# A two-bank PSUM tile split into two tiles, and 4500 added to the planned landing of a narrow job's x and sums

## The chip, the cores and the metric

The kernel runs on one core of one Trainium2 chip. The metric is device time in microseconds (us) of one execution, as the median of a few runs. Engine names are those of the profile: PE is TensorE's matmul row, PEld its weight loads, DVE VectorE, ACT ScalarE, POOL GpSimd, and SP the queue that issues every DMA of this kernel.

## The reference

Attention of 4 batches of 8 heads (576 positions, head size 64) with a decay and a causal mask feeds a block with a squared ReLU, and that feeds a block with a normalised softmax-linear unit.

```python
scores = scale * np.matmul(q, k.transpose(0, 1, 3, 2))
decay = cum[:, :, :, None] - cum[:, :, None, :]          # cum: running sum of log f
attn = softmax(where(causal, -1e9, scores + decay))
x = matmul(attn, v)                                      # to 2304 tokens x 512
h = x @ w_in                                             # 2304 x 2048
x = (s * relu(h) ** 2 + b) @ w_out                       # 2304 x 512
h = x @ w2_in                                            # 2304 x 1024
sm = softmax(h); solu = h * sm
out = (layernorm(solu) * g_ln) @ w2_out
```

## The kernel before, in words

All matrix products take float32 operands split in a high and a low part, so one product is three matmuls. The work has three stages. In the first, 16 pairs of heads go through attention: scores into PSUM (L663), minimum and exponent on DVE and ACT (L704, L750), transposes (L765), the product with v (L834). The results are stored as `xs_d`, not yet divided by the softmax sums; the inverse sums go to `rs_d`. In the second stage, the block with the squared ReLU runs in jobs. Five narrow jobs (`job`, L1076) take 256 tokens each and three of the eight slices of the hidden width; they lie between the attention's matmuls, since their matmuls have a later priority (1000 + 100 n, against the attention's running number). Wide jobs (`job_wide`, L1122) of up to 512 tokens do the rest after the attention. In the third stage pairs of tiles go through the last block (`pair2`, L1269, and `tile2_out`).

**A narrow job's input.** `x_load` (L946) issues for job n one DMA of x (512 KB, L963, into `xraw`) and two of the inverse sums, each broadcast over 64 partitions (256 KB each, L968, into `xo`, here called `rb`). A multiplication of 128x1024 elements (L971, issued by the helper at L428 or L429) joins them; it may go to DVE or POOL. Then come a store of the product (L972), the high part (L976) and the low part (L977), both written to `xhl`. `xraw`, `xo` and `xhl` each exist once, so the next job's transfers wait for this job's reads, and the next `xhl` waits for this job's first-layer matmuls (L1112, output `h`). The first narrow job (n = 0) loads in two halves.

**What sets the order.** The program records operations with `add` and then runs a planner (`Plan.run`). It plays the operations through in a modelled time, engine by engine, and writes each engine's instructions in the order in which the model starts them. On the chip each engine then works through its own list in that order and waits with semaphores. The model has a cost per operation and a lag per engine; for a transfer (L233 to L235) one modelled ring is busy for bytes over a rate, and the transfer counts as landed 900 after the ring is through, or 900 + `SLD` for those of later priority. The x and sums of a narrow job have the priority `min(b, BS)`, so they count as landed after 900. When a transfer counts as landed, its readers become ready, and an engine takes the ready operation with the least ready time plus priority. The model's times decide nothing else: no instruction waits for a clock.

**The PSUM tiles.** `hps` is one bank, `x2ps` (L364) a tile of two banks, [128, 4, 256] floats. Its halves have keys of their own in the planner, ("x2", 0, 0) and ("x2", 0, 1), so the planner treats them as independent. They serve as score banks and as targets of filler matmuls early in the attention, as the accumulator of the narrow jobs' second layer (copied out by ACT at L1101), as two of the four banks through which the wide jobs' first layer rotates (h, h1 and the two halves, L1128 to L1130; read by ACT's ReLU at L1046), and as two banks of the first `pair2`. The profile shortens both the names `x2` and, after the change, `x2h` by their numbers: the tile is `x` in the rows below. The semaphore waits themselves are set by the framework from the order of the recorded instructions and the tiles that they touch.

Of the kernel before, what the change touches and what calls it, by code (L numbers as in the profile page):

```python
# [8 lines left out]
F32 = mybir.dt.float32  # L9
# [9 lines left out]
CH = 256  # L19
# [5 lines left out]
BX = -3000  # L25
# [30 lines left out]
URGENT = -50000  # L56
SLD = 1500
SLP = 500
SLT = 100000
# [7 lines left out]
class Plan:  # L67
# [15 lines left out]

    def add(self, eng, dur, fn, r=(), w=(), pri=0, bytes=None, after=(), lk=False, rate=340, act=1.0, open=False, tiled=None, hold=0):


        ways = eng if isinstance(eng, dict) else {eng: (dur, fn)}
        ways = {e: (d[0], d[1], e == "POOL" or e == "DVE" and (lk or len(d) > 2 and d[2])) for e, d in ways.items()}
        op = dict(ways=ways, pri=pri, bytes=bytes, n=len(self.ops), succ=[], t=0.0, by=None, rate=rate, act=act, open=open, tiled=tiled, hold=hold, r=tuple(r), w=tuple(w))
        deps = set(after)  # L90
        for x in r:
            if x in self.writer:
                deps.add(self.writer[x])
        for x in w:
            if x in self.writer:
                deps.add(self.writer[x])
            deps.update(self.readers.pop(x, ()))
        for x in r:
            self.readers.setdefault(x, []).append(op["n"])
        for x in w:  # L100
            self.writer[x] = op["n"]
            self.readers.pop(x, None)
        deps.discard(op["n"])
        op["wait"] = len(deps)
        for d in deps:
            self.ops[d]["succ"].append(op["n"])
        self.ops.append(op)
        return op["n"]

    def run(self):  # L110
# [71 lines left out]
        while left:  # L182
# [4 lines left out]
            for eng in sorted(ready):  # L187
# [45 lines left out]
                if best["bytes"]:  # L233
                    ring = max(ring, t + 1300) + best["bytes"] / best["rate"]
                    end = ring + (900 if best["pri"] < BX or t < SLT else 900 + SLD)  # L235
                best["end"] = end
# [22 lines left out]
def act_p(n):  # L259
    return 51 + 0.833 * n  # L260
# [22 lines left out]
def kernel(  # L283
# [44 lines left out]
    w2_d = dram.tile([NB2, 2, 128, 1024], F32, name="w2_d")  # L328

    const = ctx.enter_context(tc.tile_pool(name="const", bufs=1))  # L330
    moe = ctx.enter_context(tc.tile_pool(name="moe", bufs=1))
# [4 lines left out]
    psa = att_st.enter_context(tc.tile_pool(name="psa", bufs=1, space=PSUM))  # L336

    def tiles(pool, shape, dt, name, n):
        return [pool.tile(shape, dt, name=f"{name}{i}") for i in range(n)]

# [22 lines left out]
    hps = [psm.tile([128, 2, CH], F32, name="h")]  # L363
    x2ps = [psm.tile([128, KD, CH], F32, name="x2")]  # L364

# [30 lines left out]
    spare = [(hps[0].rearrange("p u n -> p (u n)"), ("h", 0))]  # L396
    spare += [(x2ps[0][:, 2 * g:2 * g + 2].rearrange("p k n -> p (k n)"), ("x2", 0, g)) for g in range(2)]
    for x in ({"S": "S", "P": "PT", "O": "O"}[x] for x in SPARE):
# [14 lines left out]

    def dma(out, in_, r, w, size, pri=0, rate=340, after=()):
        add("SP", 600, lambda: nc.sync.dma_start(out=out, in_=in_), r, w, pri, bytes=size, rate=rate, after=after)

# [106 lines left out]

    P.fill = (WT, {("x2", 0, 1): zeros(x2ps[0][:, 2].rearrange("p (k n) -> p k n", k=2)), ("x2", 0, 0): zeros(x2ps[0][:, 0].rearrange("p (k n) -> p k n", k=2)), ("h", 0): zeros(hps[0][:, 0].rearrange("p (k n) -> p k n", k=2))})

# [420 lines left out]
    def x_load(n, c, src, hi, lo, khi, klo, b=BX):  # L946
# [6 lines left out]
        for g in range(2 if first else 1):  # L953
            ks = slice(2 * g, 2 * g + 2) if first else slice(0, KD)
            sz = (ks.stop - ks.start) * CH
            of = (lambda key: [key + (g,)]) if first else H
            kx, kh, kl = of(("xx", 0)), of(khi), of(klo)
            raw_, hi_, lo_ = xraw[:, ks], (lambda ks=ks: hi()[:, ks]), (lambda ks=ks: lo()[:, ks])
            if src is xs_d:
                view = xs_d[ks, :, cs].rearrange("k p t -> p k t")  # L960
                rk = [("xs", p, half) for p in range(NPAIR) for half, o, w in ((0, 0, 256), (1, 256, 320))
                      if p // PPB * S + o < t1 and p // PPB * S + o + w > t0 and ks.start <= p % PPB < ks.stop]
                dma(raw_, view, rk, kx, 512 * sz, min(b, BS))  # L963
                P.first = P.first or len(P.ops) - 1
                krb = [("xo", a, u) for a in range(2) for u in ((g,) if first else range(2))]
                rk = [x for k_ in rk for x in rs_keys(*k_[1:])]
                for a in range(2):
                    dma(rb[64 * a:64 * a + 64, ks], rs_d[ks, a, cs][None].broadcast_to((64, ks.stop - ks.start, CH)), rk,  # L968
                        [k_ for k_ in krb if k_[1] == a],
                        256 * sz, min(b, BS), rate=290)  # L970
                tt(lambda raw_=raw_: raw_, lambda raw_=raw_: raw_, lambda ks=ks: rb[:, ks], sz, ALU.mult, krb, kx, b)  # L971
                dma(xc_d[ks, :, cs].rearrange("k p t -> p k t"), raw_, kx, [("xc", c, k) for k in range(ks.start, ks.stop)],  # L972
                    512 * sz)
            else:
                dma(raw_, src[ks, :, cs].rearrange("k p t -> p k t"), [("x2d", c, k) for k in range(KD)], kx, 512 * sz, b)
            copy(hi_, lambda raw_=raw_: raw_, sz, kx, kh, b)  # L976
            tt(lo_, lambda raw_=raw_: raw_, lambda hi_=hi_: f32(hi_()), sz, ALU.subtract, kx + kh, kl, b)  # L977
# [98 lines left out]
    def job(n, c, fps, b=BMOE):  # L1076

        hi, lo, khi, klo = (lambda: xhis[0]), (lambda: xlos[0]), ("xx", 2), ("xx", 3)
        x_load(n, c, xs_d, hi, lo, khi, klo)
        kx2, x2, h, kh = ("x2", 0), (lambda: x2ps[0]), (lambda: hps[0]), ("h", 0)  # L1080
        for m, fp in enumerate(fps):
# [7 lines left out]
            for u in range(2):  # L1089
                for g in range(2):  # L1090
                    def x_mm(u=u, g=g, tb=tb, gh=gh, gl=gl, st=st, fin=fin):
                        for d in (2 * g, 2 * g + 1):
                            x_mms(x2()[:, d, :], tb, gh[:, u, :], gl[:, u, :], u, d, st and u == 0 and d % 2 == 0, fin and u == 1)

# [4 lines left out]
        for g in range(2):  # L1099
            a = slice(2 * g, 2 * g + 2)  # L1100
            add("ACT", act_p(512), lambda a=a: nc.scalar.copy(out=xo_[:, a], in_=x2()[:, a]), [kx2 + (g,)],  # L1101
                kxo[g], b)
# [19 lines left out]
    def job_wide(n, t0, width, fps, last, b=BMOE):  # L1122
# [6 lines left out]
        if x:  # L1129
            hbanks += [(lambda g=g: flat(x2ps[0][:, 2 * g:2 * g + 2]), ("x2", 0, g)) for g in range(2)]  # L1130
        work = [(m, fp, us) for m, fp in enumerate(fps) for us in ([(0,), (1,)] if x else [(0, 1)])]
# [137 lines left out]
    def pair2(g):  # L1269
# [3 lines left out]
        if g == 0:  # L1273
            banks = [(lambda i=i: late["x2w"][2 + i], ("x2w", 2 + i)) for i in range(2)]
            banks += [(lambda i=i: x2ps[0][:, 2 * i:2 * i + 2].rearrange("p k n -> p (k n)"), ("x2", 0, i)) for i in range(2)]
        else:
# [291 lines left out]
```

## Time and profile before

| | |
|---|---|
| Median of 3 runs | 793.2 us (791.77 to 794.97) |
| Profiled execution, own time | 794.93 us |
| Its span, first to last instruction | 792.9 us |
| Instructions | 12751 |
| PE busy | 773.7 us, 98% of the span |
| DVE, ACT, POOL busy | 476.5, 492.8, 132.7 us |
| Mean granted TensorE clock | 0.994 of full speed |

The span is cut in stages: attention with the narrow jobs from the start to about 272 us, wide jobs to about 589 us, the last block to the end. PE counts as busy in nearly all of it, so time is found by looking for the places where PE waits or where the granted clock is below 1.

### The profile page before, as it was taken

Reading aid. Unit: us, or ns where it says so; the run is one execution under the profiler, and the core shown is the slowest. Engines: PE = TensorE matmul, PEld = TensorE weight load, DVE = VectorE, ACT = ScalarE, POOL = GpSimd, SP = SyncE. Lnnn points to the kernel's source line nnn. Section 1 sums busy time; section 2 is a strip of 40 time slices with the busy share of each in tenths; the row PEclk is TensorE's granted clock in tenths of the full one; section 3 lists DMA queues with packets and bytes.
Section 4 is the critical chain, followed back from the end, with each engine's and each line's share of the span. In section 5 each row is a group of like instructions: output and inputs, shape, how many; then the busy total and the mean of one; then the engine's idle time right before and its main releaser. Section 6 shows DMA issues by size and latency. Waiting matters only on the chain.

```text
span 792.9 us, 12751 instructions
## 1 busy us (share of the span) xinstructions
PE 773.7 (98%) x4520; PEld 640.2 (81%) x4520; DVE 476.5 (60%) x1026; ACT 492.8 (62%) x1008; POOL 132.7 (17%) x180
## 2 busy tenths in 40 slices
PE   8998999899999999999999999999999999999998
PEld 6677788788788987888788888788997788888886
DVE  9999888688674573221378666512239966655530
ACT  7998888588777686555387676554516654443441
POOL 3332412123110020100111201100002730100000
PEclk9999999899999999999999999999999999999999
DMA  8886888886953873130467865842325121000011
GB/s 301 281 291 202 289 280 268 271 278 197 330 180 102 271 258 118 54 106 1 120 211 256 300 207 180 306 197 81 107 82 211 54 66 41 27 14 27 27 41 53
DMA packets 73015, 132.59 MB, mean 167 GB/s; under 512 B 7704, under 2 KB 29848, under 8 KB 72952
## 3 DMA queue, kind: packets, MB, share of 16 engines
q1 hardware_dynamic: 72952, 131.78, 49.6%
q8 instruction: 35, 0.57, 0.3%
q14 instruction: 28, 0.23, 0.1%
HBM read 91.17 MB, written 40.58 MB: 166 GB/s over the span
## 4 chain that ended last, share of the span: by engine, by line
PE 79%; DVE 9%; DMA 6%; issue 2%; ACT 2%; SPq 1%; POOL 0%; DVEq 0%; ACTq 0%; POOLq 0%
PE h L1112 14%; PE x L1112 9%; PE ph L1321 7%; PE x2w L1119 7%; PE x2w L1118 7%; PE x2w L1120 7%; PE po L1377 4%; PE po L1379 4%; PE po L1378 4%; PE S L663 4%; PE PT L765 3%; DMA xo<-rs_d 2%; PE O L834 2%; DVE e L704 2%; PE pt L1365 2%
## 5 line engine op out<-in xcount | busy, mean ns | idle before, releaser
L1060 DVE SCALAR_TENSOR_TENSOR gl<-r,b_sb,gh 128x512 fp32r<-128x512 f32 x71 | 54.4, 767 | 128.5 <-ACT gh L1069 114.6
L750 ACT ACTIVATE e<-e,m 128x256 f32<-128x256 f32 (+4 forms) x144 | 83.4, 582 | 10.2 <-DVE m L704 9.7
L1119 PE MATMUL x2w<-gl,u 128*128 128x512 f32 (+1 forms) x200 | 73.6, 368 | 0.0
L1120 PE MATMUL x2w<-gh,u 128*128 128x512 f32 (+1 forms) x200 | 73.6, 368 | 0.0
L1118 PE MATMUL x2w<-gh,u 128*128 128x512 f32 (+1 forms) x200 | 73.6, 368 | 0.0
L765 PE MATMUL PT<-ident,e 128*128 128x128 f32 x384 | 60.2, 284 | 3.7 <-ACT wr L869 1.3
L1046 ACT ACTIVATE r<-h 128x512 f32<-128x512 f32 x46 | 27.3, 593 | 53.7 <-PE h L1112 53.4
L1112 PE MATMUL h<-xhl,w 128*128 128x256 f32 (+1 forms) x384 | 60.0, 295 | 0.0
L1377 PE MATMUL po<-v,dh 128*128 128x512 f32 x144 | 58.2, 404 | 0.0
L1379 PE MATMUL po<-v,dl 128*128 128x512 f32 x144 | 56.3, 391 | 0.0
L765 PEld LDWEIGHTS PT<-ident,e 128*128 128x128 f32 x384 | 43.6, 143 | 15.6 <-issue 3.5
L1378 PE MATMUL po<-v,dh 128*128 128x512 f32 x144 | 56.1, 390 | 0.0
L1369 DVE TENSOR_TENSOR dl<-pt,dh 128x512 fp32r<-128x512 f32 x36 | 24.6, 689 | 49.5 <-ACT dh L1368 49.5
L1053 ACT ACTIVATE r<-r,s_sb 128x512 f32<-128x512 f32 x68 | 49.3, 725 | 2.2
L1112 PEld LDWEIGHTS h<-xhl,w 128*128 128x128 f32 x384 | 49.6, 190 | 1.2
L1112 PE MATMUL h<-xh,u 128*128 128x256 f32 (+1 forms) x216 | 46.0, 330 | 0.0
L1069 ACT ACTIVATE gh<-r,b_sb 128x512 fp32r<-128x512 f32 x62 | 44.7, 721 | 1.5 <-DVE r L1050 0.2
L1052 ACT ACTIVATE r<-r 128x512 f32<-128x512 f32 x68 | 43.0, 632 | 1.8
L1046 ACT ACTIVATE r<-x 128x512 f32<-128x512 f32 x26 | 15.5, 596 | 44.8 <-PE x L1112 44.8
L1118 PEld LDWEIGHTS x2w<-gh,u 128*128 128x128 f32 x200 | 37.7, 188 | 6.3
L1119 PEld LDWEIGHTS x2w<-gl,u 128*128 128x128 f32 x200 | 37.7, 189 | 6.2
L1120 PEld LDWEIGHTS x2w<-gh,u 128*128 128x128 f32 x200 | 37.7, 188 | 6.2
(280 smaller groups left out, 1972.4 us busy)
## 6 DMA issues: line engine op xcount, KB each, us to landing
wraw<-in_moe_w_in_dram SPq DMA_DIRECT2D x24, 512.0 KB
wraw<-in_moe_w_out_dram SPq DMA_DIRECT2D x24, 512.0 KB
w_d<-w SPq DMA_DIRECT2D x44, 256.0 KB
raw<-in_qk_dram SPq DMA_DIRECT2D x12, 608.0 KB
dec<-dec_d SPq DMA_DIRECT2D x12, 512.0 KB
v<-w_d SPq DMA_DIRECT2D x12, 512.0 KB
vs<-in_v_dram SPq DMA_DIRECT2D x16, 320.0 KB
u_d<-wr SPq DMA_DIRECT2D x20, 256.0 KB
```

Of the source, the lines that this page charges most:

```text
L750: nc.scalar.activation(out=e[:, c], in_=e[:, c], func=AF.Exp, scale=-1.0, bias=m[:, j:j + 1], accum_out=rt[:, cols[j]:cols[j] + 1])
L765: nc.tensor.transpose(pt[:, kb, :], e[:, 128 * kb:128 * kb + 128], ident)
L1053: nc.scalar.activation(out=r, in_=r, func=AF.Copy, scale=s_sb)
L1060: nc.vector.scalar_tensor_tensor(out=gl, in0=r, scalar=b_sb, in1=f32(gh), op0=ALU.add, op1=ALU.subtract)
L1112: nc.tensor.matmul(t, w_, v_[:, kc, :], start=kc == 0 and first and x == 0, stop=kc == KD - 1 and x == 2, skip_group_check=True)
L1118: nc.tensor.matmul(t, a_, gh, start=start, stop=False, skip_group_check=True)
L1119: nc.tensor.matmul(t, a_, gl, start=False, stop=False, skip_group_check=True)
L1120: nc.tensor.matmul(t, b_, gh, start=False, stop=stop, skip_group_check=True)
L1321: nc.tensor.matmul(o, s_[:, kc, :], mv[:, c], start=x < 5 and kc == 0 and z == 0, stop=kc == 1 and z == 2, skip_group_check=True)
L1377: nc.tensor.matmul(ot, dh[:, j, :], wh[:, c], start=j == 0, stop=False)
L1378: nc.tensor.matmul(ot, dh[:, j, :], wl[:, c], start=False, stop=False)
L1379: nc.tensor.matmul(ot, dl[:, j, :], wh[:, c], start=False, stop=j == 7)
```

## The change

It does two things. The two-bank tile `x2ps` becomes two tiles of one bank, `x2h0` and `x2h1`, with every use rewritten to the tile of its half. And `add` gets an argument `slack`, which the planner adds to the modelled landing of a transfer; for narrow jobs other than the first it is `SLX` = 4500 for the x and for both transfers of the sums. The instructions themselves, their sizes and their number of operands stay; the order in which the planner writes them may differ from the first of these transfers on.

```diff
+SLX = 4500
...
-    def add(self, eng, dur, fn, r=(), w=(), pri=0, bytes=None, after=(), lk=False, rate=340, act=1.0, open=False, tiled=None, hold=0):
+    def add(self, eng, dur, fn, r=(), w=(), pri=0, bytes=None, after=(), lk=False, rate=340, act=1.0, open=False, tiled=None, hold=0, slack=0):
...
                     ring = max(ring, t + 1300) + best["bytes"] / best["rate"]
-                    end = ring + (900 if best["pri"] < BX or t < SLT else 900 + SLD)
+                    end = ring + (900 if best["pri"] < BX or t < SLT else 900 + SLD) + best["slack"]
...
-    x2ps = [psm.tile([128, KD, CH], F32, name="x2")]
+    x2ps = tiles(psm, [128, 2, CH], F32, "x2h", 2)
...
-    spare += [(x2ps[0][:, 2 * g:2 * g + 2].rearrange("p k n -> p (k n)"), ("x2", 0, g)) for g in range(2)]
+    spare += [(x2ps[g].rearrange("p k n -> p (k n)"), ("x2", 0, g)) for g in range(2)]
...
-                dma(raw_, view, rk, kx, 512 * sz, min(b, BS))
+                late_ = 0 if first else SLX
+                dma(raw_, view, rk, kx, 512 * sz, min(b, BS), slack=late_)
...
-                        256 * sz, min(b, BS), rate=290)
+                        256 * sz, min(b, BS), rate=290, slack=late_)
...
-        kx2, x2, h, kh = ("x2", 0), (lambda: x2ps[0]), (lambda: hps[0]), ("h", 0)
+        kx2, x2, h, kh = ("x2", 0), (lambda d: x2ps[d // 2][:, d % 2]), (lambda: hps[0]), ("h", 0)
...
-            add("ACT", act_p(512), lambda a=a: nc.scalar.copy(out=xo_[:, a], in_=x2()[:, a]), [kx2 + (g,)],
+            add("ACT", act_p(512), lambda a=a, g=g: nc.scalar.copy(out=xo_[:, a], in_=x2ps[g]), [kx2 + (g,)],
...
-            hbanks += [(lambda g=g: flat(x2ps[0][:, 2 * g:2 * g + 2]), ("x2", 0, g)) for g in range(2)]
+            hbanks += [(lambda g=g: flat(x2ps[g]), ("x2", 0, g)) for g in range(2)]
...
-            banks += [(lambda i=i: x2ps[0][:, 2 * i:2 * i + 2].rearrange("p k n -> p (k n)"), ("x2", 0, i)) for i in range(2)]
+            banks += [(lambda i=i: x2ps[i].rearrange("p k n -> p (k n)"), ("x2", 0, i)) for i in range(2)]
```

The filler matmuls and the helper `tiles` are rewritten in the same way.

## Rows read from the trace of the kernel before

**Rows 1.** The page: busy time of each engine, and the granted clock.
```profile
PE 773.7 (98%) x4520; PEld 640.2 (81%) x4520; DVE 476.5 (60%) x1026; ACT 492.8 (62%) x1008; POOL 132.7 (17%) x180
...
PEclk9999999899999999999999999999999999999999
```

**Rows 2.** Windows by stage: start:end, length, busy by engine, PEclk, DMA share, GB/s.
```profile
90.00:140.00 50.00, 50.00 (x435) 41.65 (x435) 42.63 (x121) 42.69 (x114) 9.98 (x16) 1.00 0.85 271
...
215.00:290.00 75.00, 75.00 (x559) 64.84 (x558) 45.39 (x98) 54.45 (x122) 8.59 (x11) 1.00 0.64 204
290.00:570.00 280.00, 277.94 (x1275) 231.44 (x1274) 123.87 (x182) 168.85 (x268) 24.44 (x24) 1.00 0.48 164
```

**Rows 3.** Waits, whole span: who waited, for whom, total, times, longest.
```profile
DVE xraw L428 <- DMA xo<-rs_d: 8.5, 3, 4.0
...
PE x L1112 <- ACT r L1046: 2.1, 3, 0.7
```

**Rows 4.** Timeline of DVE: the multiplications of narrow jobs 1 to 4.
```profile
81.78 1.22 DVE L428 TENSOR_TENSOR xraw<-xraw,xo 128x1024 f32<-128x1024 f32 x1 [2.44 <-DMA xo<-rs_d]
...
143.01 1.23 DVE L428 TENSOR_TENSOR xraw<-xraw,xo 128x1024 f32<-128x1024 f32 x1 [3.98 <-DMA xo<-rs_d]
...
161.61 1.22 DVE L428 TENSOR_TENSOR xraw<-xraw,xo 128x1024 f32<-128x1024 f32 x1
...
210.08 1.35 DVE L428 TENSOR_TENSOR xraw<-xraw,xo 128x1024 f32<-128x1024 f32 x1 [2.10 <-DMA xo<-rs_d]
```

**Rows 5.** Timeline of SP: issues around job 2's multiplication.
```profile
132.08 0.38 SPq L415 DMA_DIRECT2D xraw<-xs_d  x1
132.55 1.36 SPq L415 DMA_DIRECT2D xo<-rs_d  x2
...
144.27 1.26 SPq L415 DMA_DIRECT2D xo<-rs_d  x2
145.57 0.60 SPq L415 DMA_DIRECT2D xc_d<-xraw  x1
```

**Rows 6.** Timeline of PE behind job 2's multiplication.
```profile
144.73 0.68 PE L663 MATMUL S<-qkh 64*128 64x384 f32 x1 [2.91 <-DVE m L704]
```

**Rows 7.** Windows around the three stalls, PE alone: length, PE busy, PEclk, DMA share.
```profile
82.00:90.00 8.00, 6.63 (x41) 0.79 0.94 325
140.00:152.00 12.00, 9.09 (x53) 0.72 0.74 243
210.00:214.00 4.00, 3.44 (x26) 1.00 1.04 387
```

**Rows 8.** Timeline: low part of job 2's x on DVE, and PE's first use.
```profile
145.93 1.85 DVE L428 TENSOR_TENSOR xhl<-xraw,xhl 128x1024 fp32r<-128x1024 f32 x1
...
157.55 1.19 PE L1112 MATMUL h<-xhl,w 128*128 128x256 f32 x8
```

**Rows 9.** The same two for job 1.
```profile
84.57 1.59 DVE L428 TENSOR_TENSOR xhl<-xraw,xhl 128x1024 fp32r<-128x1024 f32 x1
...
101.02 0.96 PE L1112 MATMUL h<-xhl,w 128*128 128x256 f32 x6
```

**Rows 10.** Timeline of PE and ACT in the wide jobs, three places.
```profile
307.46 0.39 PE L1112 MATMUL x<-xhl,w 128*128 128x512 f32 x1
...
307.69 0.39 PE L1112 MATMUL x<-xh,w 128*128 128x512 f32 x1
...
308.11 0.60 ACT L1046 ACTIVATE r<-x 128x512 f32<-128x512 f32 x1 [4.85 <-PE x L1112]
...
308.76 0.50 PE L1112 MATMUL x<-xh,w 128*128 128x512 f32 x1 [0.69 <-ACT r L1046]
...
396.78 1.43 PE L1112 MATMUL x<-w,u 128*128 128x512 f32 x5 [0.69 <-ACT r L1046]
...
506.56 1.65 PE L1112 MATMUL x<-w,u 128*128 128x512 f32 x6 [0.69 <-ACT r L1046]
```

**Rows 11.** Timeline of the first pair of the last block.
```profile
591.50 0.69 DVE L1306 TENSOR_TENSOR xraw<-x,wr 128x512 f32<-128x512 f32 x1 [2.06 <-PE x L1321]
...
592.98 0.73 PE L1321 MATMUL x<-v,oh 128*128 128x512 f32 x2 [0.16 <-DVE sm L1298]
```

**Rows 12.** Timeline of DVE: multiplications of the first wide jobs.
```profile
268.50 1.22 DVE L428 TENSOR_TENSOR xraw<-xraw,wraw 128x1024 f32<-128x1024 f32 x1 [0.69 <-DMA wraw<-rs_d]
...
273.56 1.23 DVE L428 TENSOR_TENSOR xraw<-xraw,wraw 128x1024 f32<-128x1024 f32 x1 [0.40 <-DMA xraw<-xs_d]
```

More of the change, by code (lines that the diff above doesn't have):

```diff
@@ L82, in __init__ @@
         self.ops, self.writer, self.readers, self.first = [], {}, {}, 0
-    def add(self, eng, dur, fn, r=(), w=(), pri=0, bytes=None, after=(), lk=False, rate=340, act=1.0, open=False, tiled=None, hold=0):
+    def add(self, eng, dur, fn, r=(), w=(), pri=0, bytes=None, after=(), lk=False, rate=340, act=1.0, open=False, tiled=None, hold=0, slack=0):
         ways = eng if isinstance(eng, dict) else {eng: (dur, fn)}
         ways = {e: (d[0], d[1], e == "POOL" or e == "DVE" and (lk or len(d) > 2 and d[2])) for e, d in ways.items()}
-        op = dict(ways=ways, pri=pri, bytes=bytes, n=len(self.ops), succ=[], t=0.0, by=None, rate=rate, act=act, open=open, tiled=tiled, hold=hold, r=tuple(r), w=tuple(w))
+        op = dict(ways=ways, pri=pri, bytes=bytes, n=len(self.ops), succ=[], t=0.0, by=None, rate=rate, act=act, open=open, tiled=tiled, hold=hold, slack=slack, r=tuple(r), w=tuple(w))
         deps = set(after)
@@ L328, with tiles @@
     w2_d = dram.tile([NB2, 2, 128, 1024], F32, name="w2_d")
+    def tiles(pool, shape, dt, name, n):
+        return [pool.tile(shape, dt, name=f"{name}{i}") for i in range(n)]
     const = ctx.enter_context(tc.tile_pool(name="const", bufs=1))
@@ L336 @@
     psa = att_st.enter_context(tc.tile_pool(name="psa", bufs=1, space=PSUM))
-    def tiles(pool, shape, dt, name, n):
-        return [pool.tile(shape, dt, name=f"{name}{i}") for i in range(n)]
     ident = const.tile([128, 128], F32, name="ident")
@@ L412, in slot, with dma @@
         return count[name] % n
-    def dma(out, in_, r, w, size, pri=0, rate=340, after=()):
-        add("SP", 600, lambda: nc.sync.dma_start(out=out, in_=in_), r, w, pri, bytes=size, rate=rate, after=after)
+    def dma(out, in_, r, w, size, pri=0, rate=340, after=(), slack=0):
+        add("SP", 600, lambda: nc.sync.dma_start(out=out, in_=in_), r, w, pri, bytes=size, rate=rate, after=after, slack=slack)
     def copy(out, in_, n, r, w, pri=0):
@@ L522, in zeros @@
                                               skip_group_check=True)
-    P.fill = (WT, {("x2", 0, 1): zeros(x2ps[0][:, 2].rearrange("p (k n) -> p k n", k=2)), ("x2", 0, 0): zeros(x2ps[0][:, 0].rearrange("p (k n) -> p k n", k=2)), ("h", 0): zeros(hps[0][:, 0].rearrange("p (k n) -> p k n", k=2))})
+    P.fill = (WT, {("x2", 0, 1): zeros(x2ps[1][:, 0].rearrange("p (k n) -> p k n", k=2)), ("x2", 0, 0): zeros(x2ps[0][:, 0].rearrange("p (k n) -> p k n", k=2)), ("h", 0): zeros(hps[0][:, 0].rearrange("p (k n) -> p k n", k=2))})
     memset("POOL", sel_, BH, 0.0, [("e", 0)], -1e5)
@@ L1092, in x_mm @@
                         for d in (2 * g, 2 * g + 1):
-                            x_mms(x2()[:, d, :], tb, gh[:, u, :], gl[:, u, :], u, d, st and u == 0 and d % 2 == 0, fin and u == 1)
+                            x_mms(x2(d), tb, gh[:, u, :], gl[:, u, :], u, d, st and u == 0 and d % 2 == 0, fin and u == 1)
                     add("PE", 6 * mm(CH), x_mm, [kgh, kgl] + wkeys(kb), [kx2 + (g,)], 1000 + 100 * n + 4 * m + 9,
```

## The prediction, made before the change was run

> **What bounds the kernel now.** I read the page first: PE is busy 98% of the span, and the granted clock stands at 9 in all slices but one, where it is 8 [rows 1]. So the kernel is a stream of matmuls, and time can be won only where PE waits or runs at the lower clock. The windows by stage say where that is not: from 90 to 140 us and from 215 to 290 us PE is busy without a gap at full clock, and from 290 to 570 us it misses 280.00 - 277.94 = 2.06 us [rows 2].
>
> The list of waits then names two things that this change touches [rows 3]. DVE waited three times, 8.5 us together, for the transfer of the sums ahead of a multiplication at L428. And PE waited three times, 2.1 us together, at L1112 for ACT's ReLU before it wrote the tile `x`.
>
> The timeline shows the first kind one by one: the multiplications of jobs 1, 2 and 4 waited 2.44, 3.98 and 2.10 us; that of job 3 not at all [rows 4]. The planner had put each at a place in DVE's list where it held the transfer for landed, and DVE takes its list in order. Behind the blocked one stands the attention's minimum (L704), and PE waits for that: the next score matmuls began at 144.73 after 2.91 us of idle, released by DVE [rows 6]. What the three stalls cost PE, by the windows around them [rows 7]: idle 8.00 - 6.63 = 1.37, 12.00 - 9.09 = 2.91 and 4.00 - 3.44 = 0.56, together 4.84 us. In the first two the mean granted clock is 0.79 and 0.72, that is, the lower of the two levels (1.2 against 2.4 GHz) for a part of the window; the lost work is 8 x 0.21 + 12 x 0.28 = 1.68 + 3.36 = 5.04 us. In the third the clock stays at 1.00. So the three stalls cost up to 9.88 us.
>
> **Part by part: the slack.** It removes no instruction. It moves, for jobs 1 to 4, the planned landing by 4.5 us, and with it everything that hangs on it: the multiplication (1.2 us on DVE), the store behind it (0.60 us of SP), the high and low part (the low part 1.85 us on DVE [rows 8]), and on SP the next job's sums, which wait for the multiplication because their buffer exists once: they were issued at 144.27, right behind it [rows 5]. Within SP's list these issues move behind others that no longer have to wait for them; I cost that at nothing, since SP had been held by the same blocked multiplication. DVE now does 4.5 us of other planned work first. The lateness to be covered is 2.44, 3.98 and 2.10 us, each under 4.5, so I take all three waits as gone; the second has only 0.5 us to spare.
>
> Does the x come too late now? Job 2's low part ended at 145.93 + 1.85 = 147.78, and PE used it first at 157.55: 9.8 us of cover [rows 8]. Without the second stall PE comes there 2.91 + 3.36 = 6.3 us sooner, the x stays where its transfer puts it, and 3.5 us are left. Job 1 has 101.02 - 86.16 = 14.9 us [rows 9]. Attention matmuls and the earlier job's second layer fill PE in between. If the cover were gone, PE would wait by what the slack exceeds it, 1.0 us for job 2.
>
> What comes out of the stalls is between 4.84 us (idle alone, if the clock falls elsewhere) and 9.88 us; I take 9.88, since PE is gap-free at full clock in the neighbouring stages of the same mix [rows 2]. What the new order costs elsewhere the trace does not show. The nearest rows are two multiplications of wide jobs whose transfers get no slack: they waited 0.69 and 0.40 us [rows 12]. So I take 1.1 us for waits that grow or appear, between a gain of 1.1 (these two vanish too) and a loss of 6.3 (a new stall of the size of the second one).
>
> Of the clock: the row shows it at 0.72 in the window of the 2.91 us idle and at 1.00 around 0.56 us of idle [rows 7]. The Trainium skill says on its page "TensorE: Matmul & The Clock Gate" (Part 1, the HAM clock gate) that how many matmuls run at the low clock varies from run to run of one kernel; by that the 5.04 us would not be there in every run, and the sum would lie up to that much higher. No view here shows a second execution, so the sum keeps the row's value and the rule is a rival's.
>
> **Part by part: the two tiles.** In the first of three places in the wide jobs, ACT's ReLU of the first half waited for PE until 308.11, although PE had by then begun the second half; the last matmuls listed before that are at 307.46 and 307.69. PE then stopped, and went on at 308.76, when the ReLU of 0.60 us had ended [rows 10]. The two halves are different banks and different keys for the planner, so the planner put the ReLU between the two groups of six matmuls of the second half; the waits treat the tile as one. With a tile for each half neither wait has a reason: 3 x 0.69 = 2.07 us, nearly all that PE misses from 290 to 570 us [rows 2]. PE carries the end here, so it counts in full. In the first `pair2` the same pattern delays DVE by 2.06 us, and PE by 0.16 us behind it [rows 11]; I take 0.16, with 2.06 as the upper bound. Copies at L1101 and the early score banks show no such wait of PE; those edits I cost at nothing, hidden by PE's own stream.
>
> **The sum.** Against the profiled execution's own 794.93 us: -9.88 (stalls) -2.07 -0.16 (tiles) +1.1 (new order) = 794.93 - 11.01 = 783.9, say **784.0 us**. That execution stands 1.7 us above the median of 793.2. I leave the 1.7 out: if the median run loses less to the stalls, there is as much less to win.
>
> **The rivals.**
> 1. *The idle goes, the clock does not come back.* The stalls' second half depends on when the clock falls, and the three runs shown already differ by 3.2 us. Then only 4.84 + 2.07 = 6.9 us are won: 788.0 us. For it: the two clock losses are as large as the idle itself. Against it: the clock is 1.00 wherever PE has no such gap. This is also the case that the page's rule above would make.
> 2. *A new wait takes the place of the largest.* Any change of landing times reorders all lists behind it, and transfers are near their limit (DMA share 0.85 from 90 to 140 us [rows 2], above 0.9 in two of the stall windows [rows 7]); another instruction may then stand in front of a late transfer, at the price of the second stall, 6.3 us: 783.9 + 6.3 = 790.2 us. Against it: the transfers that were late on DVE are the ones that get the slack.
> 3. *The slack moves nothing that matters*, because the multiplication keeps its place in DVE's list. Then only the tiles' 2.2 us are won, 792.7 us. Against it: 4.5 exceeds every wait of rows 4. The trace bears on the reason too: job 2's x and sums, 1 MB, were issued from 132.08 on and were there at 143.01, 10.9 us later [rows 4, 5]. The Trainium skill gives on "DMA: Bandwidth & Descriptors" (two cost components) a fixed 2.0 us plus bytes over 436 GB/s, by my estimate 4.4 us for 1 MB; by that the transfer would have been in time, the slack would be needless, and this rival's time would hold. The trace disagrees, and decides.
> 4. *Slower: the x is late for PE.* Place: the first L1112 matmuls of jobs 1 to 4. It decides if the cover shrinks to nothing, that is, if the new plan uses the x the moment it holds it for landed. Price: 4.5 us of idle in four jobs, 18 us: 783.9 + 18 = 801.9 us. For it: job 2's cover shrinks to 3.5 us. Against it: job 1 has 14.9 us, and narrow jobs yield to attention.
>
> **How the numbers follow.** The forecast gets 0.48, with a range of its own from 779.5 (no new waits, the upper bound in `pair2`, and the median's 1.7 taken off as well: 794.93 - 9.88 - 2.07 - 2.06 - 1.7 = 779.2) to 787. Rival 1 gets 0.19, rival 2 0.19, rival 3 0.05, rival 4 0.09. A measurement of this kernel can tell some 0.5% from no change, 4.0 us: faster is below 789.2, slower above 797.2. Faster is the forecast and rival 1, 0.67, and 0.02 of rival 2, whose time lies at the edge: 0.69. The same is the rest of rival 2 and rival 3, 0.22. Slower is rival 4, 0.09. The range is 779.5 to 793.0: it takes in rivals 1 to 3, and leaves out rival 4 and the tails of the forecast.
>
> **What would show it.** Right: no wait of a few us of DVE's L428 for `xo<-rs_d`; the granted clock at 9 in every slice; no idle of 0.69 us of PE at L1112 for ACT in the wide jobs, and PE busy over the whole of that stage; ACT's ReLU of one half starting while PE still writes the other. The slack's step is wrong if L428 still waits, or if PE's idle between 60 and 215 us stays near 5 us with another releaser; the tile step is wrong if the 0.69 us idles remain. The prediction as a whole fails if the first L1112 matmuls of a narrow job wait for DVE or a DMA.

## The result, and the profile after

The changed kernel takes 788.12 us (median of 5, 786.29 to 789.9) against 793.36 us of the kernel before (median of 5, 791.77 to 794.97): a ratio on record of 0.9916, 95% interval 0.9893 to 0.9939. Run a second time, beside experiments, it came to 787.22 us and 0.9902 (0.9881 to 0.9923). So it is faster: by 5.2 and 7.9 us as the medians go, by 6.7 and 7.8 us as the ratios go. 784.0 us was predicted, and the range of 779.5 to 793.0 holds the result; the forecast's own range, which ended at 787, does not. By time alone the result lies on the first rival's 788.0.

On the page of the execution after, of 788.12 us, the slice with an 8 in the clock row is gone, and PE is busy 2.4 us less than in [rows 1]. Its span is 786.3 us, so PE idles 786.3 - 771.3 = 15.0 us; before it was 792.9 - 773.7 = 19.2 us.

```profile
PE 771.3 (98%) x4522; PEld 639.9 (81%) x4522; DVE 483.2 (61%) x1039; ACT 489.2 (62%) x998; POOL 132.3 (17%) x176
...
PEclk9999999999999999999999999999999999999999
```

The timeline of DVE shows the four multiplications of narrow jobs 1 to 4, now without a bracket: none waits for the sums, where three did in [rows 4].

```profile
85.64 1.21 DVE L429 TENSOR_TENSOR xraw<-xraw,xo 128x1024 f32<-128x1024 f32 x1
...
146.60 1.23 DVE L429 TENSOR_TENSOR xraw<-xraw,xo 128x1024 f32<-128x1024 f32 x1
...
167.65 1.25 DVE L429 TENSOR_TENSOR xraw<-xraw,xo 128x1024 f32<-128x1024 f32 x1
...
205.61 1.22 DVE L429 TENSOR_TENSOR xraw<-xraw,xo 128x1024 f32<-128x1024 f32 x1
```

The windows of PE after (start:end, length, busy, granted clock, DMA share, GB/s) answer to [rows 2, 7]:

```profile
80.00:90.00 10.00, 9.86 (x80) 1.00 0.99 345
90.00:100.00 10.00, 8.28 (x54) 0.83 0.64 228
...
140.00:152.00 12.00, 12.00 (x107) 1.00 0.97 263
...
205.00:215.00 10.00, 10.00 (x84) 1.00 0.90 267
215.00:290.00 75.00, 73.77 (x534) 1.00 0.61 203
290.00:570.00 280.00, 280.00 (x1301) 1.00 0.47 158
```

In the windows of the three old stalls PE's idle is down from 4.84 to 0.14 us, and the wide jobs are full. But two stretches that had no gap now have one: 1.72 us from 90 to 100, with the clock at 0.83 there, and 1.23 us from 215 to 290. What stands behind the first is in the timelines of POOL, DVE and PE:

```profile
90.98 2.79 POOL L430 TENSOR_TENSOR qk<-raw,qkh 128x1216 fp32r<-128x1216 f32 x1
...
91.15 3.16 DVE L877 SCALAR_TENSOR_TENSOR wr<-wraw,wr 128x512 uint32<-128x512 uint32 x1
...
95.13 0.74 PE L664 MATMUL S<-qkh 128*128 128x288 f32 x2 [1.55 <-DVE m L705]
```

In the new order the subtraction of 128x1216 elements stands on POOL; in the order before it was on DVE, 1.41 us. On DVE an instruction of a form that else takes 0.69 us began 0.17 us after POOL's, took 3.16, and ended 0.54 us after POOL (90.98 + 2.79 = 93.77; 91.15 + 3.16 = 94.31). Behind it stand the minima (L705), and PE waited 1.55 us for one of them.

**Where the time went, by checkpoints.** The same matmuls can be found in every trace, so their starting times show where a kernel is ahead. The columns give the start of the first wide job's `h` with 128x512 outputs, of the first matmul with operand `u`, of the first of `pair2` and of the first with output `po`, and the end of the last matmul, in us from the start of the span.

| execution | first wide | first `u` | `pair2` | `po` | end |
|---|---|---|---|---|---|
| before | 268.00 | 337.45 | 571.41 | 620.85 | 788.95 |
| after | 264.23 | 333.28 | 565.27 | 614.39 | 782.43 |
| after, second run | 261.18 | 329.39 | 561.38 | 610.50 | 778.54 |
| two tiles only | 265.81 | 334.02 | 566.01 | 615.11 | 783.15 |
| slack only | 261.80 | 331.96 | 565.91 | 615.36 | 783.47 |

After, the narrow jobs' stage ends 3.77 us sooner, the wide jobs add 2.37, the first `pair2` 0.32, the rest 0.06: 6.52 us. The 2.37 hold a new wait: at 266.48, right behind the first wide matmul, PE stands 0.58 us for DVE. Without it, as in the second run, the wide jobs give 3.21.

### The profile page after: what moved, and what is told of

The parts are those of the page before. It is cut to its first block, busy times and chain, and to the rows that moved or that the text cites. A ratio compares the mean times of both kernels' runs of the same rounds, so it can differ in the third digit from the quotient of the medians.

```text
span 786.3 us, 12750 instructions
## 1 busy us (share of the span) xinstructions
PE 771.3 (98%) x4522; PEld 639.9 (81%) x4522; DVE 483.2 (61%) x1039; ACT 489.2 (62%) x998; POOL 132.3 (17%) x176
## 4 chain that ended last, share of the span: by engine, by line
PE 81%; DVE 9%; ACT 3%; issue 3%; DMA 3%; SPq 1%; POOL 0%; ACTq 0%; POOLq 0%; DVEq 0%
PE h L1114 14%; PE x2h L1114 9%; PE ph L1323 7%; PE x2w L1122 7%; PE x2w L1121 7%; PE x2w L1120 7%; PE S L664 4%; PE po L1381 4%; PE po L1379 4%; PE po L1380 4%; PE PT L766 4%; PE O L835 3%; PE pt L1367 2%; DVE e L705 2%; PE PT L835 1%
## 5 line engine op out<-in xcount | busy, mean ns | idle before, releaser
L1062 DVE SCALAR_TENSOR_TENSOR gl<-r,b_sb,gh 128x512 fp32r<-128x512 f32 x72 | 56.2, 781 | 137.5 <-ACT gh L1071 123.3
L1048 ACT ACTIVATE r<-x2h 128x512 f32<-128x512 f32 x26 | 15.5, 597 | 42.1 <-PE x2h L1114 42.1
```

The source lines that it names most:

```text
L1062: nc.vector.scalar_tensor_tensor(out=gl, in0=r, scalar=b_sb, in1=f32(gh), op0=ALU.add, op1=ALU.subtract)
```

## The experiments

Twelve runs were made in three groups of four, each group on a chip of its own beside the kernel before. All ratios are to the kernel before in the same group, so kernels of different groups are compared by ratio. The edits are shown against the changed kernel; `...` marks lines left out. Theory A is: the gain is the three multiplication stalls and the 0.69 us waits, less the stall at 91 us. Theory B: the new order as a whole decides, by luck. Theory C: the clock that an idle costs is not the same in every execution.

| kernel | median, us | ratio, 95% interval |
|---|---|---|
| two tiles only | 789.22 | 0.9941 (0.9929 to 0.9954) |
| slack only | 789.57 | 0.9939 (0.9923 to 0.9956) |
| both, one subtraction on DVE | 785.5 | 0.9885 (0.9872 to 0.9899) |
| two tiles, slack for job 3 only | 793.02 | 0.9977 (0.9958 to 0.9996) |
| the changed kernel again | 787.22 | 0.9902 (0.9881 to 0.9923) |
| both, one subtraction on DVE, again | 786.28 | 0.9882 (0.9861 to 0.9902) |
| two tiles, multiplications late | 789.78 | 0.9926 (0.9905 to 0.9947) |
| two tiles, one subtraction on POOL | 792.67 | 0.9958 (0.9939 to 0.9978) |
| slack 2500 | 792.65 | 0.9966 (0.9944 to 0.9987) |
| slack 7000 | 788.95 | 0.9923 (0.9894 to 0.9952) |
| slack 14000 | 794.6 | 0.9992 (0.9968 to 1.0015) |
| slack for job 2 only | 788.76 | 0.9916 (0.989 to 0.9943) |

### Two tiles only

```diff
-SLX = 4500
+SLX = 0
```

> Only the tile is split; the slack is 0, so every engine has the instruction order of the kernel before. Theory (the two halves of one tile wait for each other): the three idles of 0.69 us of PE at the first-layer matmuls of the wide jobs are gone, the three waits of DVE for the sums stay (2 to 4 us each); the time falls by 2.1 to 2.3 us, to some 791.2. Rival (the waits of 0.69 us have another cause): they stay, and the time is that of before, 793.4.

It gave 789.22 us, 0.9941: 4.7 us by the ratio, over twice the predicted 2.2. All engines work in the order of before, and DVE still waits for the sums, 8.6 us in three places. The two executions can be compared matmul by matmul. The timeline of PE before, at the first `u` and the first `pair2`:

```profile
337.45 0.39 PE L1112 MATMUL h<-xh,u 128*128 128x512 f32 x1
...
571.41 0.63 PE L1321 MATMUL x2w<-w,oh 128*128 128x512 f32 x2
```

and the same two matmuls with two tiles:

```profile
334.02 0.39 PE L1114 MATMUL h<-xh,u 128*128 128x512 f32 x1
...
566.01 0.63 PE L1323 MATMUL x2w<-w,oh 128*128 128x512 f32 x2
```

Between them lie 233.96 us before and 231.99 with two tiles, 1.97 us less. Just two of the three 0.69 us waits of [rows 10] lie there, those at 396.78 and 506.56. So one costs 0.985 us, not 0.69; the first, at 308.76, moves the two executions apart by as much (0.98). The reason can be read in the timeline: matmuls of this size take 0.39 us each but start 0.227 us apart (337.45, 337.68, 337.91). The idle of a row is counted from the end of the last one, so what they else overlap is lost on top: before the wait of [rows 10] lie 308.76 - 307.69 = 1.07 us from start to start, 0.84 more than 0.227, and the first matmul behind it is slow too (0.34 us to the next start). In the changed kernel, in its second run and with two tiles only this stretch is 231.99 us long, to the hundredth; with the slack alone it is 233.95. In the first `pair2`, the stretch to the first `po` falls from 49.44 to 49.10 us, 0.34, where 0.16 was predicted. Three waits and this make 3.3 us. The 2.2 us by which this execution leads at the first wide matmul stand beside no row of the tiles: the order is the same and PE idles behind late sums here too (1.47 us at 84, 2.25 us at 143). But this execution's mean granted clock is 0.998, that of before's profiled one 0.994. What the ratio's 4.7 us hold above 3.3 is left open; the higher clock (0.998 on average over its five executions, 0.996 over the 17 of the kernel before beside them) is likely a part of it.

### Slack only

```diff
-    x2ps = tiles(psm, [128, 2, CH], F32, "x2h", 2)
+    x2two = psm.tile([128, KD, CH], F32, name="x2")
+    x2ps = [x2two[:, 0:2], x2two[:, 2:4]]
```

> Only the slack; the two halves are slices of one two-bank tile as before, and every engine has the instruction order of the changed kernel. Theory (the two parts add up): the waits of DVE for the sums are gone, idles of 0.69 us at the wide jobs' first layer are back, and the time lies 2.1 us above the changed kernel's 788.1, near 790.2. Rival (the new order has no place where one half waits for the other, so the split is worth nothing in it): 788.1.

It gave 789.57 us, 0.9939, in the order of the changed kernel. No multiplication waits; PE's misses from 290 to 570 are back (277.94 us busy). At the first wide matmul this execution is 6.2 us ahead, and it loses 0.7 of it again. PE idles in new places, in its timeline:

```profile
85.67 0.28 PE L689 MATMUL O<-ident,R 128*9 128x128 f32 x1 [1.27 <-ACT xt L426]
95.75 0.41 PE L767 MATMUL PT<-ident,e 128*128 128x128 f32 x2 [1.34 <-DVE pb L775]
...
250.18 3.14 PE L1115 MATMUL h<-xhl,w 128*128 128x256 f32 x24 [1.47 <-ACT r L1049]
264.19 0.38 PE L1122 MATMUL x<-gl,w 128*128 128x256 f32 x1 [0.72 <-DVE gl L1063]
```

So the slack alone is worth about as much as the tiles alone. Their sum would be 9.5 us by the ratios; together they give 6.7 and 7.8 in two runs outside this group.

### Both, with the subtraction of 91 us on DVE

```diff
-        tt(lambda: t, lambda: r, lambda: f32(h()), n, ALU.subtract, kr + kh, kt, b)
+        sub = lambda: nc.vector.tensor_tensor(out=t, in0=r, in1=f32(h()), op=ALU.subtract)
+        add({"DVE": (dve(n), sub, True), "POOL": (pool2(n), sub)}, 0, 0, kr + kh, kt, b)
```

One instruction moves from POOL to DVE; the order is else the changed kernel's.

> The changed kernel with one instruction moved: the subtraction of 128x1216 elements for the low part of one pair's q and k, which the new order gives to POOL at 91 us, is issued to DVE at the same place; all other orders stay. Theory (in the changed kernel a DVE instruction takes 3.16 us instead of 0.69 because POOL's subtraction of 2.79 us runs beside it, and PE idles 1.55 us behind it and then runs at a low clock): DVE needs 1.4 + 0.7 = 2.1 us for both, one less than now; PE's idle there shrinks from 1.55 to about 0.5 us, the granted clock stays high, and 1 to 3 us of 788.1 are won: 785 to 787. Rival (the long DVE instruction is not POOL's doing, or PE waits there for something else): the idle stays or grows by DVE's extra 1.4 us, 788 to 790.

785.5 us, 0.9885. In the timelines of DVE and PE, the instruction that took 3.16 us takes 0.68, and the subtraction 1.41; PE's wait behind them falls from 1.55 to 0.41 us:

```profile
91.98 0.68 DVE L878 SCALAR_TENSOR_TENSOR wr<-wraw,wr 128x512 uint32<-128x512 uint32 x1
92.58 1.41 DVE L558 TENSOR_TENSOR qk<-raw,qkh 128x1216 fp32r<-128x1216 f32 x1
...
94.81 0.74 PE L665 MATMUL S<-qkh 128*128 128x288 f32 x2 [0.41 <-DVE m L706]
```

Then it ran again with the changed kernel on the same chip.

> The changed kernel itself, beside the three runs below, so that all are compared on one chip. Theory A (what the change gives is the three multiplication stalls and the three 0.69 us waits, less a new stall at 91 us where DVE's wr instruction took 3.16 us beside POOL's 2.79 us subtraction): 0.991 to 0.993 of the kernel before, DVE's wr row near 91 us again at 2.5 to 3.5 us with PE idle right behind it. Theory B (the gain is luck of the new planned order): the same ratio, so this run alone decides nothing. Theory C (an idle's clock penalty is not repeatable): the mean granted clock lies at 0.997 to 1.000 and the time does not follow it.

> The changed kernel with the one 128x1216 subtraction that stood on POOL at 91 us put on DVE, a second time, next to the changed kernel on the same chip. Theory A: 2.0 to 3.0 us under the changed kernel (DVE's wr row back at 0.7 us, PE busy 9.4 us or more of the 10 us from 90 to 100), so 0.988 to 0.9895 of the kernel before. Theory B: within 1 us of the changed kernel, the earlier 785.5 us being chance.

0.9902, just under the 0.991 to 0.993 expected, and 0.9882; in the changed kernel the row was at 3.17 us once more, with 1.58 us of idle behind it. The median is 0.9 us lower with the subtraction on DVE, under the 2 to 3 expected and inside theory B's 1 us, and the intervals overlap. In both groups it is the fastest kernel, but the times do not separate it from the changed one. The rows show the collision; its price for the whole is 0.9 us by these medians and 1.6 by these ratios, which is not clear of the noise.

### The collision added to the order of before

```diff
-SLX = 4500
+SLX = 0
...
-        tt(lambda: t, lambda: r, lambda: f32(h()), n, ALU.subtract, kr + kh, kt, b)
+        pool = lambda: nc.gpsimd.tensor_tensor(out=t, in0=r, in1=f32(h()), op=ALU.subtract)
+        sub = pool if p == 9 else lambda: nc.vector.tensor_tensor(out=t, in0=r, in1=f32(h()), op=ALU.subtract)
+        add({"DVE": (dve(n), sub, True), "POOL": (pool2(n), pool)}, 0, 0, kr + kh, kt, b)
```

> Two PSUM tiles with the order of before, and one instruction moved: the 128x1216 subtraction that DVE does in 1.41 us at 91 us goes to POOL, as the changed kernel has it. Theory A: POOL takes 2.5 to 3.1 us for it, the next DVE instruction that touches SBUF alone (wr, or the 128x9 R) stands until POOL is done, 1.5 us or more in place of 0.7 or 0.16, and PE idles 0.3 to 1.5 us behind it: 0.5 to 2.5 us above the two-tile kernel's 789.2 us. Theory B (the two engines do not hinder each other and the 3.16 us row came from its own order): the DVE rows keep 0.7 and 0.16 us, DVE is 1.4 us ahead, and the time is 788 to 789.5 us.

792.67 us, above the expected top of 791.7, and yet not by the mechanism expected: beside POOL's work DVE read PSUM and waited 1.12 us for PE, and `wr` met only the last 0.37 us of it.

```profile
89.73 2.80 POOL L558 TENSOR_TENSOR qk<-raw,qkh 128x1216 fp32r<-128x1216 f32 x1 [1.53 <-ACT qkh L419]
...
92.16 0.92 DVE L879 SCALAR_TENSOR_TENSOR wr<-wraw,wr 128x512 uint32<-128x512 uint32 x1
...
211.25 1.36 PE L666 MATMUL S<-qkh 64*128 64x384 f32 x2 [1.95 <-DVE m L707]
```

The old stalls at 143 (3.00 us) and 211 us (1.95) are there, larger than with two tiles alone (2.25 and 0.36). Its mean granted clock over 12 executions is 0.996. So this run does not price the collision. Whether the moved instruction is the cause of the longer stalls 50 and 120 us further on was not tested.

### The multiplications late, nothing else

Each of the later multiplications, with what follows from it alone, is written some 4.5 us of planned time further back in its queue; PE's order is that of before.

```diff
-SLX = 4500
+SLX = 0
+LATE = 4500
...
-                fn()
+                emit(best, fn, t)
...
-                tt(lambda raw_=raw_: raw_, lambda raw_=raw_: raw_, lambda ks=ks: rb[:, ks], sz, ALU.mult, krb, kx, b)
+                tt(lambda raw_=raw_: raw_, lambda raw_=raw_: raw_, lambda ks=ks: rb[:, ks], sz, ALU.mult, krb, kx, b, late=0 if first else LATE)
```

(`emit` holds such an operation, and those that depend on a held one, until the planner's clock has passed its time plus `late`.)

> Two PSUM tiles, and the order of before, except that each of the three later jobs' multiplications, with what follows from it alone, stands some 4.5 us of planned time further back in its queue. Nothing else is reordered: PE's order is that of before. Theory A: the multiplications' waits fall under 1.5 us in total, PE's idle of 1.5, 2.3 and 0.8 us (84, 143 and 213 us of the two-tile kernel with the order of before) goes, and the time is 3.5 to 5.5 us under that kernel's 789.2: 783.7 to 785.7 us, 0.987 to 0.989 of the kernel before. Theory B (the planned order as a whole carries the gain, not the place of the multiplications): 788 to 790 us. Theory D (a multiplication that stands later makes its x late for PE): PE waits for xhl's consumers before the first L1114 matmuls of a job, and the time is over 790 us.

789.78 us, 0.9926: theory A's 0.987 to 0.989 was missed, theory B's 788 to 790 us met. The multiplications' waits are gone but for 0.41 us, and PE idles where it did, from 140 to 152 us, for another reason. Timelines of ACT, DVE and PE:

```profile
146.58 0.66 ACT L888 ACTIVATE wr<-wraw 128x512 f32<-128x512 f32 x1 [2.37 <-DMA wraw<-in_moe_w_in_dram]
...
148.69 1.23 DVE L447 TENSOR_TENSOR xhl<-xraw,xhl 128x1024 fp32r<-128x1024 f32 x1 [2.00 <-ACT xhl L437]
...
149.32 0.55 PE L784 MATMUL PT<-ident,e 128*128 128x128 f32 x3 [1.59 <-ACT e L769]
```

ACT waited 2.37 us for a weight transfer, so the high part of x, next in its list, came late; DVE stood 2.00 us before the low part; PE's transposes waited for the exponents behind that. This is the second rival's mechanism, a new wait in place of the largest. So to take the multiplications' waits away is not enough by itself: here the high part moved behind another late transfer. That a new plan of what follows on ACT and DVE is what makes the slack better than this is an argument, not shown.

### The slack for one job, and other sizes

For job 3, whose multiplication had not waited, and, with `n == 2`, for job 2, whose had waited longest (two tiles in both):

```diff
-                late_ = 0 if first else SLX
+                late_ = SLX if n == 3 else 0
```

> Split tiles, and the slack for narrow job 3 alone, whose multiplication had not waited in the kernel before. Theory (the slack is worth the waits that it takes away): nothing is taken away, the three waits of jobs 1, 2 and 4 stay in some form, and the time is that of the split alone, some 791.2, give or take what a reordering from 160 us on brings by chance (1 us either way). Rival (it is the reordering and not the waits that made the changed kernel faster): it moves by several us from 791.2, as far as 788.

> The changed kernel with the slack for the second job's transfers alone, the ones whose multiplication waited longest (3.98 us before). Theory A: that wait goes, the waits of job 1 and job 4 (2.4 and 2.1 us before) stay, with 0.5 to 1.5 us of PE idle behind each, so the time lies between that of two tiles alone (0.994) and of the changed kernel with the subtraction on DVE (0.988): 786 to 789.5 us. Theory B: as with the slack for job 3 alone (0.998), the new order costs what the wait gave: 790 to 794 us.

Job 3 alone: 0.9977 and 793.02 us, worse than either theory expected; the waits stay (8.3 us in three), and the run costs about 3 us against two tiles alone. Its mean granted clock is 0.9964, that of two tiles alone 0.998, so a part of the 3 us is the clock, and the rest is put down to the new order. Job 2 alone: 0.9916, as good as the changed kernel and within theory A's range. Its own wait is gone, job 4's stays (2.15 us), and job 1's, expected to stay, is not there. Job 3's multiplication, which had hardly waited, now waits for its x, in the timelines of DVE and PE:

```profile
164.03 1.23 DVE L429 TENSOR_TENSOR xraw<-xraw,xo 128x1024 f32<-128x1024 f32 x1 [3.24 <-DMA xraw<-xs_d]
...
167.41 0.75 PE L664 MATMUL S<-qkh 128*128 128x288 f32 x2 [2.38 <-DVE m L705]
```

Then the size, in the changed kernel (each of these orders has the subtraction of 91 us on DVE):

```diff
-SLX = 4500
+SLX = 2500
```

> The changed kernel with the slack at 2500 in place of 4500. Its planned order has the 128x1216 subtraction of 91 us on DVE. Theory A (a slack helps once it is as long as the lateness, and that was 2.44, 3.98 and 2.10 us in the kernel before): the multiplication that was 3.98 us late still waits about 1.5 us, the two others under 0.5; PE idles 1 to 1.5 us more there than in the changed kernel with the subtraction on DVE (786.3 us), so 786 to 788.5 us, 0.988 to 0.9915 of the kernel before. Theory B (the order that happens to come out decides, not the slack): the time lies anywhere from 784 to 794 us and its PE idle does not stand beside the multiplications.

> The changed kernel with the slack at 7000 in place of 4500; the subtraction of 91 us is on DVE here too. Theory A: no multiplication waits for xo<-rs_d, none of x is late for PE (the rows of before leave 11.6 and 16.5 us between x's last write and its first use, 2.5 us more slack takes from that), and it lies with the changed kernel with the subtraction on DVE: 784.5 to 787.5 us, 0.9865 to 0.990. Theory B: 2 us or more away from that, with idle at places that have nothing to do with the multiplications.

> The changed kernel with the slack at 14000, so that the cost feared in the prediction's fourth rival (x late for PE) is provoked. Theory A: PE waits 0 to 2.5 us before the first L1114 matmuls of each later job, or works at the next job's scores meanwhile; 785 to 791 us. Rival 4 as it was priced (PE waits for x in each of the three jobs): over 795 us. Theory B: anywhere.

2500: 0.9966, above theory A's range. One multiplication waits still, job 4's, for 3.66 us, not job 2's for 1.5. 7000: 0.9923, no multiplication waits for the sums, 1.5 us above the top of theory A's range. 14000: 794.6 us, 0.9992, nothing won, above theory A's 785 to 791. Its multiplications do not wait for the sums either, and the fourth rival's place shows only a trace of its mechanism, at the first `h` matmul of job 1:

```profile
100.33 1.57 PE L1114 MATMUL h<-xhl,w 128*128 128x256 f32 x11 [0.32 <-DVE xhl L429]
```

So an order in which no multiplication waits for the sums can still be as slow as before. Theory B holds that far: three of the orders with slack (job 3, 2500, 14000) came out above the order with none (0.9941), though for 2500 the intervals overlap. Theory A holds for the changed kernel and its variant with the subtraction on DVE, where the rows show the waits gone and the time follows. Why 2500 and 14000 lose what they do stays open. The checkpoints say this much: 14000 is 5.4 us behind two tiles alone at the first `u` (339.44 against 334.02) and no further behind at the end (788.58 against 783.15), so its loss lies ahead of that matmul. The traced execution of 2500 shows no loss at all (783.48 at the end); it was the fastest of twelve.

## Why the prediction held, and where its sum was off

**The two tiles: right in place, the size too small.** All three 0.69 us idles are gone, and PE is full from 290 to 570 us. At the first of the three places ACT's ReLU now runs beside PE's next writes to the other half (timelines of ACT and PE after):

```profile
303.56 0.60 ACT L1048 ACTIVATE r<-x2h 128x512 f32<-128x512 f32 x1 [3.49 <-PE x2h L1114]
303.58 0.39 PE L1114 MATMUL x2h<-xhl,w 128*128 128x512 f32 x1
303.81 0.62 PE L1114 MATMUL x2h<-xh,w 128*128 128x512 f32 x2
```

The term was 2.07 + 0.16; measured are 3 x 0.985 + 0.34 = 3.3 us. The step that failed is to take the idle of a row for its cost.

**The slack's waits: right, but one stall was a draw.** All three waits of DVE are gone, and with them 4.7 of the 4.84 us idle. By the prediction's own sign this is less clean: PE's idle from 60 to 215 us was 7.17 us before, not 5, and is 4.25 now, near the 5 us that were to speak against the step; 1.72 of it is the new stall at 95 us, and 2.21 lie from 60 to 82 us, where 2.09 were before. The x is not late, by the timelines of DVE and PE after:

```profile
149.63 1.21 DVE L429 TENSOR_TENSOR xhl<-xraw,xhl 128x1024 fp32r<-128x1024 f32 x1
...
153.54 0.88 PE L1114 MATMUL h<-xhl,w 128*128 128x256 f32 x6
```

Job 2's low part ends at 149.63 + 1.21 = 150.84, 2.7 us before its first use, where 3.5 were predicted. Rivals 3 and 4 fall.

That the first stall belongs to this order was read from one execution. Up to 82 us every engine has the same order before, with two tiles only, with the subtraction on POOL, and with the slack for job 3 or job 2 alone. Job 1's multiplication waited 2.44 us before ([rows 4]); in the other four, in this order:

```profile
81.77 1.23 DVE L429 TENSOR_TENSOR xraw<-xraw,xo 128x1024 f32<-128x1024 f32 x1 [2.81 <-DMA xo<-rs_d]
...
81.21 1.23 DVE L429 TENSOR_TENSOR xraw<-xraw,xo 128x1024 f32<-128x1024 f32 x1 [0.32 <-DMA xo<-rs_d]
...
80.74 1.23 DVE L429 TENSOR_TENSOR xraw<-xraw,xo 128x1024 f32<-128x1024 f32 x1 [0.47 <-DMA xo<-rs_d]
...
81.02 1.22 DVE L429 TENSOR_TENSOR xraw<-xraw,xo 128x1024 f32<-128x1024 f32 x1
```

PE's idle from 82 to 90 us was 1.37, 1.76, 0.05, 0.06 and 0.27 us in these five. So 1.37 + 1.68 = 3.05 of the predicted 9.88 us were one execution's, and missing in three of five. Job 2's wait is there each time that its transfers have no slack: 3.98, 3.31, 4.07 and 3.62 us.

**The new order: the price too low.** For waits that appear 1.1 us were taken. Measured are 1.72 us of idle from 90 to 100 and 1.23 from 215 to 290, 2.95 us, with the clock at 0.83 in the first. The largest is one that no row of before could show, since POOL had no such instruction there. The second rival had foreseen a new stall, at 6.3 us, but by an instruction in front of a late transfer; here it is DVE beside POOL, and less than half of the price in idle.

**The clock: the term that missed most.** 5.04 us were read from one execution. The kernel before ran 59 times beside the experiments, with a mean granted clock of 0.993 to 1.000, on average 0.9967. The 8 executions at 1.000 took 792.9 us on average, the 19 at 0.995 or less 796.4. A straight line through all 59 gives 0.56 us per 0.001, with a correlation of -0.61; the three groups alone give 0.18 to 0.83. So the clock counts, but the profiled execution, at 0.994, was one of the lowest, and by these means about half of its loss is there in the middle of the runs. The changed kernel's 11 executions average 0.9986: 0.0019 higher, by that line 1.1 us (an estimate; 0.3 to 1.6 by the lines of the groups), not 5.04.

The part of a stall that is the clock is not the same in every execution. Windows of PE show it in pairs. From 82 to 90 us, two tiles only had more idle than the kernel before in [rows 7] and kept the full clock, where before fell to 0.79; from 90 to 100 us, the changed kernel's second run had the stall of 1.6 us and kept the full clock, where the first run fell to 0.83 (one window of each of these two runs):

```profile
82.00:90.00 8.00, 6.24 (x50) 1.00 0.90 315
...
90.00:100.00 10.00, 8.38 (x71) 1.00 0.67 234
```

The Trainium skill says on "TensorE: Matmul & The Clock Gate" (Part 1) that how many matmuls run at the low clock at the start of one kernel varies from run to run. The runs here agree, and show it behind stalls in the middle of a kernel too.

**The sum, and luck in it.** With the terms as the traces show them, the clock by the estimate, the gain is 4.7 (stalls) + 3.3 (tiles) - 2.95 (new idle) + 1.1 (clock) = 6.2 us, against 5.2 to 7.9 measured; 11.0 were predicted. The first rival had the right condition in part, a clock that gives little back. That its 788.0 us met the result is luck: it took the tiles too low by 1.2 us, left out the 2.95 us of new waits, and counted no gain of the clock. The clock is not the whole of the gain either: in the second group, on one chip, the three executions of each kernel at 1.000 average 791.9 us before and 785.8 us after, 6.1 us apart.

The forecast, too, can be met by one pair of executions. The changed kernel's second profiled run, with the clock at 1.000 the fastest of its 11, took 784.24 us, against 794.93 of the profiled execution before, which stands at the top of its group's 791.77 to 794.97:

| stretch | predicted | after | after, second run |
|---|---|---|---|
| to the first wide matmul | -9.88 + 1.1 = -8.78 | -3.77 | -6.82 |
| wide jobs | -2.07 | -2.37 | -3.21 |
| first `pair2` | -0.16 | -0.32 | -0.32 |
| rest | 0 | -0.06 | -0.06 |
| all, against before's 794.93 | -11.01 | -6.52 | -10.41 |

Against one execution with a low clock, one with a full clock is 10.4 us ahead, and even there the parts differ: 2.0 us less than predicted ahead of the wide jobs, 1.3 us more behind. Over all executions the change is worth 5.2 to 7.9 us.

## What to carry to other kernels

Do not read a clock loss, or the length of a wait for a transfer, from one profiled execution: look at the granted clock of all the runs first, count only the difference of the means, and look for the wait in a second trace of the same order. The cost of a short wait of a pipelined engine is the distance between starts less the usual one, not the idle that the row shows (0.985 against 0.69 us here). When a planner is told that a transfer lands later, it writes another order, and that order is a draw of its own, here between 0.9902 and 0.9992 of the kernel before: list what stands on which engine in the new order, above all what moved to POOL, and try a few values.

## What the runs showed of the hardware

A DVE instruction that works in SBUF alone stood while POOL did its subtraction. Two such rows bear on the times above: `wr` at 3.16 us in place of 0.69, ending behind POOL's instruction; and with the slack only, a `TENSOR_SCALAR` on 128x9 elements at 1.67 us in place of 0.17. The trace after has more, such as `gl` at 114.54, 1.32 us in place of 0.75, ending 0.55 us after a POOL instruction of 1.27 us that began at 114.04. The reverse is seen too: at 291.43 a POOL instruction took 1.34 us, and 0.62 the next time, beside a DVE subtraction at 291.61 that kept its 0.69. In the second case above DVE's instructions that read PSUM ran beside POOL before that at their usual times (0.28 and 0.41 us). The timelines of POOL and DVE with the slack only:

```profile
91.65 3.12 POOL L431 TENSOR_TENSOR qk<-raw,qkh 128x1216 fp32r<-128x1216 f32 x1
...
92.79 0.41 DVE L706 CUSTOM_DVE_ANT_1 e<-S,dec 128x256 f32<-128x256 f32 x1
...
93.14 1.67 DVE L685 TENSOR_SCALAR R<-R 128x9 f32<-128x9 f32 x1
```

The small one ended at 93.14 + 1.67 = 94.81, POOL at 91.65 + 3.12 = 94.77. The Trainium skill's page "SBUF — State Buffer" (SBUF: two separate sides) says that the two engines share a pair of ports, that of a POOL instruction and a DVE instruction in a two-port mode, or with two inputs in SBUF, the one to start first has it for its whole instruction, and that the other is blocked. The two rows agree. At 291 it was POOL that stood, though its row begins first; DVE was then still at the instruction before. The planner also keeps such instructions apart, but in its own modelled time; on the chip they met.
